# Attention backward for one query: PSUM pools put together, narrower add matmuls, ef matmuls emitted by double units, small stores batched

## The chip, the cores and the metric

The kernel runs on one core of a Trainium2 chip. The metric is device time in microseconds (us), median of several runs. The kernel before takes 953.49 us over 13 runs (951.75 to 955.58). "PE" is the matmul engine (TensorE), "PEld" its weight load, "DVE" the vector engine, "ACT" the scalar engine, "SP" the engine that issues DMA. Runs are labelled fast or slow (slow here: over 1.5% above the fastest run of the same kernel). The "granted clock" is the share of its full speed at which PE was let run, as the trace records it.

## The reference

One query per head against 8192 keys, 32 heads, head size 128, bf16; the output and the gradients of q, k and v.

```python
def _fwd_reference(q, k, v):            # q (1,32,1,128), k and v (1,32,8192,128)
    scale = q.shape[-1] ** -0.5
    scores = jnp.einsum('bhqd,bhkd->bhqk', q, k) * scale
    attn = _softmax(scores, axis=-1)
    return jnp.einsum('bhqk,bhkd->bhqd', attn, v)

def reference(q, k, v, grad_out):       # forward value, then the gradients of q, k, v
    ...
```

k and v are read once (134 MB together) and their gradients written once (134 MB).

## The kernel before

A head needs these steps. DVE multiplies the tile of k by q (`prod`, 4.4 us) and adds the two halves of each row (`h1`, 2.3 us). PE adds the remaining 64 columns with an identity matrix ("adds", output `sp`), and DVE reduces that to the scores. The same is done for v and grad_out. Then comes the softmax: a maximum over partitions with a matmul, `exp` on ACT, a sum with a matmul, a reciprocal. The probabilities and score gradients are put into padded tiles (`ap`, `dp`) and transposed by PE (`tp`). "cd" are 128 small matmuls that give the output and the gradient of q. "ef" are 32 matmuls of 4 rows each whose results, copied from PSUM by ACT, are the gradients of v and k.

The parts that the change and the argument touch (cuts marked by `...`):

```python
    NB = 4                                   # columns per row and add matmul
    ps_sp, ps_tp, ps_cd, ps_st = ...         # four PSUM pools, bufs=1, one bank each
    ps_ef = ctx.enter_context(tc.tile_pool(name="ps_ef", bufs=2, space=bass.MemoryType.PSUM))  # 2 banks each

    def emit_ef_unit(h, u):
        ...
        r = 2 * half + rr
        ef = ps_ef.tile([P, 2, 4 * D], F32, tag="ef")
        for ti in range(2):
            t = 2 * tpair + ti
            nc.tensor.matmul(
                ef[:, ti, :], lhsT=d["adT"][32 * t:32 * t + 4, which, r, :],
                rhs=bd[32 * t:32 * t + 4, :, :],
                start=True, stop=True, tile_position=(32 * t, 0),
            )
        ...
        nc.scalar.activation(out=ost[...], in_=ef[...], func=ACT.Copy)

    for i in range(H + 1):
        ...
        for u in range(4):
            if prv is not None:
                emit_ef_unit(prv, u)                  # two ef matmuls, then 32 cd matmuls
                emit_cd(prv, u // 2, 2 * (u % 2))
                emit_cd(prv, u // 2, 2 * (u % 2) + 1)
        ...
```

The framework reorders: each engine's order of issue comes from a scheduler, not from the text.

## Time and profile before

| | share of the span |
|---|---|
| PE busy | 77% |
| DVE busy | 60% |
| ACT busy | 54% |
| granted PE clock, mean | 0.61 of full speed |
| DMA | 285 GB/s, with stretches of over 400 |

First, lines of the page of before: its span, the busy times (us, share, count of instructions), and the chain of waits by engine.

```profile
span 951.7 us, 15184 instructions
...
PE 728.5 (77%) x6592; PEld 321.1 (34%) x6592; DVE 566.8 (60%) x680; ACT 517.4 (54%) x577; POOL 4.5 (0%) x18
...
PE 49%; DVE 31%; issue 6%; ACT 4%; ACTq 0%; DVEq 0%
```

No engine is full, and the chain changes hands between PE and DVE: it is a loop of waits. The timeline of a middle head (start us, duration us, engine, line, what, and in brackets the idle time ahead with its releaser) shows it:

```profile
477.19 0.29 DVE L164 TENSOR_REDUCE nb<-stt 128x1 f32<-128x128 f32 x1 [1.09 <-PE stt L158]
...
477.40 4.41 DVE L113 TENSOR_TENSOR prod<-kt,qb_all 128x8192 bf16<-128x8192 bf16 x1
...
482.07 2.28 DVE L117 TENSOR_TENSOR h<-prod 128x4096 bf16<-128x4096 bf16 x1
...
484.40 3.57 PE L127 MATMUL sp<-h,ident_bf 128*128 128x256 bf16 x16 [4.81 <-DVE h L117]
...
487.91 0.61 PE L254 MATMUL ef<-gbd,adT 4*128 4x512 bf16 x4
...
497.54 0.61 PE L254 MATMUL ef<-qbd,adT 4*128 4x512 bf16 x2
...
502.94 0.42 DVE L231 COPY cd_sb<-cd 128x256 f32<-128x256 f32 x1 [4.33 <-PE cd L221]
```

DVE leads from 477.2 to 484.4 us while PE runs out of work (4.81 us idle before the adds). Then PE leads for 22 us. The copy of cd comes every 29.38 us (473.56, then 502.94).

PE's busy time within that head by line (window, length, PE busy, PEld busy, granted clock, DMA share, GB/s), in the order ef, cd, adds:

```profile
473.50:502.90 29.40, 9.12 (x32) 1.65 (x32) 0.56 0.71 286
473.50:502.90 29.40, 5.49 (x130) 2.61 (x128) 0.56 0.71 286
473.50:502.90 29.40, 7.63 (x33) 4.42 (x33) 0.56 0.71 286
```

### The profile page before, as it was taken

What the parts mean: (1) busy time and instruction counts of PE and PEld (TensorE: products, weight loads), DVE (VectorE), ACT (ScalarE), POOL (GpSimd) and SP (SyncE); (2) the same over time, 40 slices, a digit from 0 to 9 for tenths busy, and PEclk for the clock granted to TensorE, in tenths of its full rate; (3) what the DMA queues carried; (4) which work ended last, traced back from release to release, by engine and by line L of the source; (5) the groups of instructions that cost most, each with busy time, mean ns of one, the idle gap of its engine ahead of it and who ended that gap; (6) DMA issues with size and microseconds to landing.
All of it is one profiled execution on the core that took longest, in us unless ns stands there. A gap on an engine that the chain in (4) does not pass through costs nothing.

```text
span 951.7 us, 15184 instructions
## 1 busy us (share of the span) xinstructions
PE 728.5 (77%) x6592; PEld 321.1 (34%) x6592; DVE 566.8 (60%) x680; ACT 517.4 (54%) x577; POOL 4.5 (0%) x18
## 2 busy tenths in 40 slices
PE   1598777797777977788777788677797678877696
PEld 0343333343333333333333333333343333333331
DVE  6967775556764567655576555675556765557610
ACT  0066644665445654456554465544565445654487
POOL 1000000000000000000000000000000000000000
PEclk9999655655555555555555555655555655656655
DMA  9588987667777667776677766777767777667355
GB/s 397 220 288 311 377 352 309 274 268 294 292 289 299 253 289 310 287 306 257 274 292 308 310 259 273 287 292 305 288 256 296 299 286 306 256 274 304 127 222 227
DMA packets 28130, 271.52 MB, mean 285 GB/s; under 512 B 3232, under 2 KB 3232, under 8 KB 3232
## 3 DMA queue, kind: packets, MB, share of 16 engines
q1 hardware_dynamic: 27920, 269.51, 70.3%
q8 instruction: 51, 0.84, 0.4%
q10 hardware_dynamic: 144, 1.05, 0.3%
q14 instruction: 15, 0.12, 0.0%
HBM read 136.31 MB, written 134.23 MB: 284 GB/s over the span
## 4 chain that ended last, share of the span: by engine, by line
PE 49%; DVE 31%; issue 6%; ACT 4%; ACTq 0%; DVEq 0%
DVE prod L113 23%; PE ef L254 21%; PE cd L221 14%; PE sp L127 5%; DVE h L117 4%; ACT ost L260 4%; PE stt L232 3%; PE tp L208 2%; PE tp L206 2%; PE stt L158 1%; PE stt L178 1%; DVE nb L164 1%; DVE eda L176 1%; DVE zt L177 0%; DVE ndl L186 0%
## 5 line engine op out<-in xcount | busy, mean ns | idle before, releaser
L260 ACT ACTIVATE ost<-ef 128x1024 bf16<-128x1024 f32 x512 | 505.3, 1025 | 299.9 <-PE ef L254 286.7
L127 PE MATMUL sp<-h,ident_bf 128*128 128x256 bf16 x1024 | 239.1, 400 | 162.5 <-DVE h L117 161.0
L127 PEld LDWEIGHTS <-ident_bf 128*128 128x128 bf16 x1024 | 134.4, 136 | 259.3 <-issue 207.1
L254 PE MATMUL ef<-qbd,adT 4*128 4x512 bf16 x512 | 149.4, 575 | 27.9 <-ACT ost L260 27.0
L117 DVE TENSOR_TENSOR h<-prod 128x4096 bf16<-128x4096 bf16 x64 | 146.0, 2281 | 0.0
L113 DVE TENSOR_TENSOR prod<-kt,qb_all 128x8192 bf16<-128x8192 bf16 x32 | 141.3, 4415 | 3.4 <-DMA kt<-in_k_dram 3.4
L113 DVE TENSOR_TENSOR prod<-vt,gb_all 128x8192 bf16<-128x8192 bf16 x32 | 141.4, 4417 | 0.0
L254 PE MATMUL ef<-gbd,adT 4*128 4x512 bf16 x512 | 134.3, 583 | 2.4 <-ACT ost L260 2.0
L254 PEld LDWEIGHTS <-adT 4*128 4x128 bf16 x1024 | 51.9, 98 | 168.0 <-issue 162.5
L231 DVE COPY cd_sb<-cd 128x256 f32<-128x256 f32 x32 | 13.6, 424 | 133.7 <-PE cd L221 133.7
L144 DVE TENSOR_TENSOR qbd<-mask,qb_all 128x512 bf16<-128x512 bf16 x32 | 13.6, 425 | 89.8 <-PE ef L254 89.8
L210 DVE COPY adT<-tp 128x1024 bf16<-128x1024 bf16 x32 | 22.1, 691 | 41.6 <-PE tp L208 41.6
L234 DVE CAST orow<-stt 1x256 bf16<-1x256 f32 x32 | 13.2, 412 | 48.5 <-PE stt L232 48.5
L232 PE MATMUL stt<-cd_sb,sel_f 128*1 128x256 f32 x64 | 31.9, 601 | 0.0
L221 PE MATMUL cd<-vt,ap__136 128*1 128x128 bf16 x704 | 31.7, 295 | 0.0
L221 PE MATMUL cd<-vt,ap__132 128*1 128x128 bf16 x704 | 31.5, 296 | 0.0
L178 PE MATMUL stt<-zt,ones_f 128*128 128x2 f32 x64 | 15.8, 317 | 19.5 <-DVE zt L177 19.5
L221 PE MATMUL cd<-kt,dp__138 128*1 128x128 bf16 x704 | 30.4, 301 | 0.0
L221 PE MATMUL cd<-kt,dp__134 128*1 128x128 bf16 x704 | 30.3, 301 | 0.0
L221 PE MATMUL cd<-vt,ap__140 128*1 128x128 bf16 x640 | 27.8, 288 | 0.0
L221 PE MATMUL cd<-kt,dp__142 128*1 128x128 bf16 x640 | 27.3, 292 | 0.2 <-issue 0.2
L164 DVE TENSOR_REDUCE nb<-stt 128x1 f32<-128x128 f32 x32 | 9.3, 289 | 29.6 <-PE stt L158 29.5
(278 smaller groups left out, 337.2 us busy)
## 6 DMA issues: line engine op xcount, KB each, us to landing
out_dram<-ost SPq DMA_DIRECT2D x128, 1024.0 KB, 3.9
kt<-in_k_dram SPq DMA_DIRECT2D x32, 2048.0 KB, 15.0
vt<-in_v_dram SPq DMA_DIRECT2D x32, 2048.0 KB, 12.3
gb_all<-in_grad_out_dram ACTq DMA_DIRECT2D x1, 1024.0 KB
qb_all<-in_q_dram SPq DMA_DIRECT2D x1, 1024.0 KB
out_dram<-orow SPq DMA_DIRECT2D x64, 0.2 KB
```

The source lines that it names most:

```text
L113: nc.vector.tensor_tensor(out=prod[:], in0=xt[:], in1=wb[:, h, :].unsqueeze(1).to_broadcast([P, J, D]), op=ALU.mult)
L117: nc.vector.tensor_tensor(out=h1[:], in0=prod[:, :, 0:DH], in1=prod[:, :, DH:D], op=ALU.add)
L127: nc.tensor.matmul(d["sp"][:, which, :, :], lhsT=ident_bf[:], rhs=prod[:, :, a * NB:(a + 1) * NB], start=(a == 0), stop=(a == NA - 1),)
L164: nc.vector.tensor_reduce(out=nb[:], in_=stt[:, 0:P], axis=AX.X, op=ALU.max, negate=True)
L178: nc.tensor.matmul(stt[:, P:P + 2], lhsT=ones_f[:], rhs=zt[:], start=True, stop=True)
L206: nc.tensor.transpose(tp[:, 0, r, :], apad[:, r, :], ident_bf[:])
L208: nc.tensor.transpose(tp[:, 1, r, :], dpad[:, r, :], ident_bf[:])
L210: nc.vector.tensor_copy(out=adT[:], in_=tp[:])
L221: nc.tensor.matmul(cd[32 * jj:32 * jj + 1, which * D:(which + 1) * D], lhsT=pad[:, r, c:c + 1], rhs=xt[:, j, :], start=(r == 0 and t == 0) ...
L232: nc.tensor.matmul(d["st"][0:1, 256:512], lhsT=sel_f[:], rhs=cd_sb[:], start=True, stop=True)
L254: nc.tensor.matmul(ef[:, ti, :], lhsT=d["adT"][32 * t:32 * t + 4, which, r, :], rhs=bd[32 * t:32 * t + 4, :, :], start=True, stop=True, ti ...
L260: nc.scalar.activation(out=ost[:, j0:j0 + 8, :].rearrange("p j d -> p (j d)"), in_=ef[:].rearrange("p a n -> p (a n)"), func=ACT.Copy,)
```

## The change

Its intent is to free PSUM banks for a third ef buffer, to emit ef matmuls four at a time, and to drop 64 stores of 256 bytes. The scores' sums and cd now share one bank (`pa`), the transposes and statistics another (`pb`). To make the scores' sums fit, an add matmul has 128 columns instead of 256, so there are twice as many.

```diff
-    NB = 4
+    NB = 2
-    ps_sp, ps_tp, ps_cd, ps_st ...   (four pools, bufs=1)
-    ps_ef = ... bufs=2
+    ps_ab = ... bufs=1
+    ps_ef = ... bufs=3
+    pa = ps_ab.tile([P, 512], F32, tag="pa")
+    sp_v = pa[:, 0:2 * J * NB].rearrange("p (w j b) -> p w j b", w=2, b=NB)
+    cd = pa[:, 256:512]
+    pb = ps_ab.tile([P, 512], F32, tag="pb")          # transposes, statistics
+    outT = consts.tile([P, 2, H], F32, tag="outT")    # both small outputs, stored once at the end
...
-        nc.tensor.matmul(d["st"][0:1, 256:512], lhsT=sel_f[:], rhs=cd_sb[:], start=True, stop=True)
-        ... two stores of 256 bytes per head
+        for w_ in range(2):
+            nc.tensor.matmul(pb[:, 384 + w_:385 + w_], lhsT=cd_sb[:, w_ * D:(w_ + 1) * D], rhs=sel_f[:], ...)
+        nc.vector.tensor_copy(out=outT[:, :, h], in_=pb[:, 384:386])
...
-    def emit_ef_unit(h, u):          # two matmuls, one buffer
+    def emit_ef_du(h, du):           # four matmuls, two buffers, then two evictions
+        for tpair in range(2):
+            ef = ps_ef.tile([P, 2, 4 * D], F32, tag="ef")
+            for ti in range(2):
+                t = 2 * tpair + ti
+                nc.tensor.matmul(ef[:, ti, :], ..., tile_position=(32 * t, 0))
+        for tpair in range(2):
+            nc.scalar.activation(...)
...
+            for du in range(2):
+                emit_ef_du(prv, du)
+                for r in range(4):
+                    emit_cd(prv, du, r)               # 64 cd matmuls in a row
```

The transposes of `dp` now wait for the copy of those of `ap`, since both use the same part of `pb`.

## The prediction

> **What bounds the kernel now.** No engine is full: the page gives PE 77%, DVE 60%, ACT 54% of 951.7 us, and DMA moves 285 GB/s where single stretches reach over 410. The chain of waits says a loop: PE 49%, DVE 31%. A middle head in the timeline (473.5 to 502.9 us, 29.4 us per head) splits into DVE-only work of 7.2 us (nb, product of k, reduce, half-add, while PE idles 4.8 us until the half-add ends) and 22.2 us of PE (adds, ef, transposes, cd, adds). PE runs at granted clock 0.5 almost throughout. Copies of cd come 28.4 us apart on average, since early heads have a better order.
>
> **What the change does.**
> - Adds: 64 matmuls of 128 columns per head for 32 of 256. Columns are equal. The trace spaces 256-column adds 223 ns (3.57 us for 16); the Trainium skill ("TensorE: Matmul & The Clock Gate", Back-to-back issue gap) says N/1.2 ns cold, 213, and the trace agrees within 5%. Transposes, also 128 columns with a 128-column weight load each, come every 135 ns. So a pair of small adds should cost 225 to 270 ns: 0 to +1.5 us of PE per head.
> - Reductions read half as much: 0.42 to about 0.29 us, twice per head.
> - The sum over cd: one matmul pair of 0.94 us becomes two with full-width f32 weights; the 128x2 f32 matmul of the statistics takes 0.52, so about 1.04: no gain.
> - 64 tiny stores vanish. They are in no chain: about 0.
> - A third ef buffer: "PE ef waits for ACT ost" is 29 us in total; at most that.
> - sp and cd now share one bank, tp and statistics another. The skill ("PSUM — Partial Sum Buffer", Terms) says PE and DVE may not touch one bank and quadrant at once; so dependencies order them (no run shows the collision itself). This, and the new emission, changes the static order, which I read from the built program.
>
> **The new loop, per head**, counted with durations of the trace from the last cd matmul: ef, cd sum and 32 adds of s, with interleaved ef: 7.1 to 7.9 us. Then DVE alone leads: reduce 0.3, half-add 2.25, max, product of v 4.4, dmx, reduce, half-add 2.25, nb: to about 17.7. Exp now stands on ACT behind all eight ef evictions of dk (1.025 us each), which end at 17 to 19.4. Exp, eda, zt: 0.8. Then the next product of k, 4.4 us, stands in DVE's order ahead of the reciprocal that only needs the sum, so the transposes start at 23.5 to 25.2 while PE idles some 4 us. Transposes with a copy between, 8 us with cd and four ef pairs. Period 31 to 33.3 us against 28.4: both products and both half-adds (13.3 us) are now in series with s-adds, softmax and cd, where before about half were hidden behind PE.
>
> First cd ends at about 54 us as before; 31 periods of 32.2, less 9 in the last heads without products, plus 15 of tail: about 1055 us.
>
> **Prediction:** 1050 us, range 1000 to 1090; faster by over 2%: 0.05, within 2%: 0.05, slower by over 2%: 0.90.
>
> **What would show it.** PE idle per head rising from 5 to 8-10 us, in two gaps: before the transposes (on ap, behind the product of k) and before the statistics matmul (on zt). Exp waiting with ACT busy until just before. Chain: DVE share above 45%. Adds 112 to 135 ns apart. "PE ef waits for ACT ost" falling or unchanged. DVE waits before cd_sb remaining.
>
> **What would make it wrong.** A PE clock at full speed for long after the denser adds (period below 30); adds of 4-byte runs slower than 135 ns; k or v loads arriving late (then longer).

## More of the kernel before

`tile_position=(32 * t, 0)` puts a matmul on one of four row groups of the array.

## The result

The changed kernel takes 911.07 us (907.95 to 917.35, 8 runs); the ratio to before is 0.956 (95% interval 0.9538 to 0.9581). A ratio is the mean time of one kernel's fast runs over that of the other's fast runs in the same rounds, so not quite the ratio of the medians quoted here. The prediction, 1050 us, was wrong, and wrong in sign.

The page of after, the same lines where it has them:

```profile
span 906.1 us, 17304 instructions
...
PE 629.7 (69%) x7682; PEld 410.0 (45%) x7682; DVE 567.4 (63%) x715; ACT 501.6 (55%) x577; POOL 4.5 (1%) x18
...
PE 3%; ACT 1%; DVE 0%; ACTq 0%; issue 0%; DVEq 0%
```

The chain of waits stops early here (its shares sum to some 4%), so it can't be compared; the timeline has to do. One head of after, from one copy of cd to the next (488.96 to 516.26). Down to 504.15 the lines are of this head; from 478.16 on they are the steps of the head before it, which this head repeats:

```profile
488.96 0.42 DVE L230 COPY cd_sb<-pa 128x256 f32<-128x256 f32 x1 [3.66 <-PE pa L220]
...
489.44 0.61 PE L232 MATMUL pb<-sel_f,cd_sb 128*128 128x1 f32 x4 [0.21 <-DVE cd_sb L230]
...
489.90 1.04 PE L128 MATMUL pa<-h,ident_bf 128*128 128x128 bf16 x8
...
493.61 1.04 PE L128 MATMUL pa<-h,ident_bf 128*128 128x128 bf16 x8
...
494.69 0.29 DVE L136 TENSOR_REDUCE t__5634<-pa 128x64 f32<-128x128 f32 x1 [0.50 <-PE pa L128]
...
497.23 4.42 DVE L116 TENSOR_TENSOR prod<-vt,gb_all 128x8192 bf16<-128x8192 bf16 x1
...
504.15 0.28 DVE L165 TENSOR_REDUCE nb<-pb 128x1 f32<-128x128 f32 x1
...
478.16 4.41 DVE L116 TENSOR_TENSOR prod<-kt,qb_all 128x8192 bf16<-128x8192 bf16 x1
...
478.39 0.56 PE L179 MATMUL pb<-zt,ones_f 128*128 128x2 f32 x2 [2.33 <-DVE zt L178]
...
483.13 0.61 PE L208 MATMUL pb<-ident_bf,ap__127 128*128 128x128 bf16 x4 [4.18 <-DVE ap__127 L192]
...
484.77 0.61 PE L254 MATMUL ef<-gbd,adT 4*128 4x512 bf16 x4
...
485.32 1.55 PE L220 MATMUL pa<-vt,ap__127 128*1 128x128 bf16 x51
...
487.34 1.55 PE L220 MATMUL pa<-kt,dp__129 128*1 128x128 bf16 x64
...
488.83 0.39 PE L254 MATMUL ef<-gbd,adT 4*128 4x512 bf16 x3
```

The static order is just the one that the prediction read from the built program: DVE goes through reduction, half-add, product of v and nb in one piece, then the product of k stands ahead of the reciprocal, and PE waits for the transposes. Here are that wait and the one on the statistics matmul, totals over the run (who waited for what: us, times, longest):

```profile
PE pb L179 <- DVE zt L178: 79.2, 32, 8.7
...
PE pb L208 <- DVE ap__123 L192: 42.5, 11, 4.2
PE pb L208 <- DVE ap__127 L192: 42.1, 11, 4.2
PE pb L208 <- DVE ap__131 L192: 41.8, 10, 4.2
...
PE ef L254 <- ACT ost L261: 33.2, 67, 0.5
```

The new wait ahead of the transposes is 126 us in all, 4.2 us in a head like this one. But the copies of cd come every 27.31 us (this one, then 488.96 above), not every 32.2:

```profile
461.65 0.42 DVE L230 COPY cd_sb<-pa 128x256 f32<-128x256 f32 x1 [3.66 <-PE pa L220]
```

Cut into the prediction's own terms, with the times of the lines above:

| stretch of a head | predicted, us | measured, us |
|---|---|---|
| last cd matmul to end of the adds of s | 7.1 to 7.9 | 5.7 (488.9 to 494.6) |
| end of the adds to end of nb | 9.8 to 10.6 | 9.8 (494.65 to 504.43) |
| end of nb to product of k | 0.8 to 2.5 | 1.0 (477.13 to 478.16) |
| product of k to transposes | 5.0 | 5.0 (478.16 to 483.13) |
| transposes to last cd matmul | 8 | 5.7 (483.13 to 488.83) |

The second and third row are worked out from the points of time that the prediction gives (17.7 for the end of nb; 17 to 19.4 for ACT, and 0.8 more). The terms in which DVE leads lie in the predicted ranges, two of them at the low end. The two stretches in which PE leads were oversized by some 4 us together. PE's busy time by line in one head of after, in the order ef, cd, adds:

```profile
461.65:488.96 27.31, 6.00 (x35) 1.21 (x32) 0.63 0.79 308
461.65:488.96 27.31, 3.69 (x128) 2.93 (x128) 0.63 0.79 308
461.65:488.96 27.31, 8.05 (x64) 6.53 (x64) 0.63 0.79 308
```

Against before, ef fell from 9.12 to 6.00 us, cd from 5.49 to 3.69, and the adds rose from 7.63 to 8.05. In after, what follows four ef matmuls starts 0.54 to 0.55 us after them (484.77 to 485.32, 486.80 to 487.34), where in before two took as long (497.54 to 498.07).

### The profile page after: what moved, and what is told of

It reads as the page before. It is cut to its first block, busy times and chain, and to the rows that moved or that the text cites. A ratio compares the mean times of both kernels' runs of the same rounds, so it can differ in the third digit from the quotient of the medians.

```text
span 906.1 us, 17304 instructions
## 1 busy us (share of the span) xinstructions
PE 629.7 (69%) x7682; PEld 410.0 (45%) x7682; DVE 567.4 (63%) x715; ACT 501.6 (55%) x577; POOL 4.5 (1%) x18
## 5 line engine op out<-in xcount | busy, mean ns | idle before, releaser
L128 PE MATMUL pa<-h,ident_bf 128*128 128x128 bf16 x2048 | 257.3, 288 | 23.0 <-DVE h L120 23.0
L128 PEld LDWEIGHTS <-ident_bf 128*128 128x128 bf16 x2048 | 209.6, 120 | 83.4 <-issue 81.8
L254 PE MATMUL ef<-qbd,adT 4*128 4x512 bf16 x512 | 110.4, 471 | 33.2 <-ACT ost L261 33.2
L254 PE MATMUL ef<-gbd,adT 4*128 4x512 bf16 x512 | 84.8, 550 | 0.0
L179 PE MATMUL pb<-zt,ones_f 128*128 128x2 f32 x64 | 17.7, 346 | 79.2 <-DVE zt L178 79.2
L209 DVE COPY adT<-pb 128x512 bf16<-128x512 bf16 x64 | 27.2, 425 | 29.2 <-PE pb L208 29.2
L208 PE MATMUL pb<-ident_bf,ap__123 128*128 128x128 bf16 x44 | 6.7, 308 | 42.5 <-DVE ap__123 L192 42.5
L208 PE MATMUL pb<-ident_bf,ap__127 128*128 128x128 bf16 x44 | 6.7, 308 | 42.1 <-DVE ap__127 L192 42.1
L208 PE MATMUL pb<-ident_bf,ap__131 128*128 128x128 bf16 x40 | 6.1, 308 | 41.8 <-DVE ap__131 L192 41.8
L159 PE MATMUL pb<-dmx,ones_f 128*128 128x128 f32 x64 | 25.4, 500 | 0.9 <-DVE dmx L157 0.9
L232 PE MATMUL pb<-sel_f,cd_sb 128*128 128x1 f32 x128 | 19.8, 259 | 6.7 <-DVE cd_sb L230 6.7
L220 PE MATMUL pa<-vt,ap__127 128*1 128x128 bf16 x704 | 24.0, 306 | 0.0
L220 PE MATMUL pa<-vt,ap__123 128*1 128x128 bf16 x704 | 23.5, 307 | 0.0
```

The lines of the kernel that those rows point to most:

```text
L128: nc.tensor.matmul(d["sp"][:, which, :, :], lhsT=ident_bf[:], rhs=prod[:, :, a * NB:(a + 1) * NB], start=(a == 0), stop=(a == NA - 1),)
L159: nc.tensor.matmul(stt[:, 0:P], lhsT=ones_f[:], rhs=dmx[:], start=True, stop=True)
L179: nc.tensor.matmul(stt[:, P:P + 2], lhsT=ones_f[:], rhs=zt[:], start=True, stop=True)
L208: nc.tensor.transpose(tp_v[:, r, :], pad_[:, r, :], ident_bf[:])
L209: nc.vector.tensor_copy(out=adT[:, w_, :, :], in_=tp_v)
L220: nc.tensor.matmul(cd[32 * jj:32 * jj + 1, which * D:(which + 1) * D], lhsT=pad[:, r, c:c + 1], rhs=xt[:, j, :], start=(r == 0 and t == 0) ...
```

## The experiments

Theory Q: four ef matmuls that stand next to each other on PE and sit on four different row groups run at the same time, so a four costs what a two cost. The prediction costed each two at 0.54 us. The Trainium skill ("TensorE: Matmul & The Clock Gate", Part 3: Packing small matmuls — row/col tiling) says that matmuls on different row groups run concurrently; the trace of after agrees, 0.54 us for four. Rivals: the third ef buffer as such or the batched stores (B), a higher granted clock under the denser adds (C), the emission by itself (E).

### The same kernel with two row groups used twice

```diff
-        for tpair in range(2):                  # t = 0,1 then 2,3 of one r
-            ef = ps_ef.tile(...)
+        for rr in range(2):                     # t, t+1 of r, then t, t+1 of r + 1
+            r = 2 * half + rr
+            ef = ps_ef.tile(...)
```

> The kernel after, with one edit: the four ef matmuls of a double unit use two row groups of the array twice (tiles t, t+1 of two r) instead of four row groups once. Same counts, same order on PE, DVE and ACT, same buffers. Theory Q (four ef matmuls in different row groups run at once, 0.54 us for four instead of 0.54 for two): each run of four costs 1.06 us, about 2 us more per head on the PE stretches that lead, up to 3 with the ACT queue behind it: 970 to 1000 us. Rival B (the gain comes from the third ef buffer, the batched stores or the shorter reductions): unchanged, 905 to 917. Rival C (the gain comes from a higher granted clock under the denser adds): unchanged, 905 to 920, clock 0.64 as before.

Measured: 1003.14 us, ratio to before 1.052 (1.0496 to 1.0544). The order on all engines is that of after: in the built programs no instruction of PE, DVE, ACT or SP stands elsewhere. In its timeline:

```profile
473.57 1.03 PE L254 MATMUL ef<-gbd,adT 4*128 4x512 bf16 x4
...
474.54 1.55 PE L220 MATMUL pa<-vt,ap__131 128*1 128x128 bf16 x51
...
476.02 1.03 PE L254 MATMUL ef<-gbd,adT 4*128 4x512 bf16 x4
...
476.99 1.88 PE L220 MATMUL pa<-kt,dp__133 128*1 128x128 bf16 x64
```

A four now takes 0.97 us (473.57 to 474.54) instead of 0.54. Rivals B and C fall as causes by themselves: buffers, stores and adds were untouched, and 92 us came back. The time is even 3 us over the expected range. One thing was not expected: the run of 64 cd matmuls takes 1.81 us here (476.99 to 478.80) and 1.49 in after, though it wasn't edited. That is the granted clock, taken up below: the edit took away the fours, and the raised clock went with them. So not all of the 92 us is the fours; the table under "Why the prediction was wrong" divides them.

### New pools, old emission

```diff
-    emit_ef_du, loop by double units            (as in after)
+    emit_ef_unit, loop by single units          (as in before, with eight 128-column adds for four of 256)
```

> The kernel after (pools, 128-column adds, batched stores) with the old emission of ef units one by one, cd and adds in between; the static order of DVE is that of after, on PE ef comes in twos and cd in runs of 16 to 32. Theory Q: as slow as or a little slower than a_noquad, 975 to 1010 us, that is slower than before: without the fours, the shared bank alone loses. Rival B: 905 to 920.

Measured: 1009.09 us, ratio 1.0584 (1.0568 to 1.0601). The shared banks, narrower adds, third buffer and batched stores together, without the fours, are slower than before. This is close to what the prediction described.

### Old pools, new emission

```diff
-    emit_ef_unit, loop by single units
+    emit_ef_du, loop by double units            (all else as in before)
```

> The kernel before (five pools, two ef buffers, 256-column adds, small stores) with the new emission alone. The built program keeps the order of before: ef in twos between runs of 14 cd matmuls, since the scheduler spreads them when only two ef buffers exist and cd has its own bank. Theory Q: the emission alone brings nothing: 940 to 960 us. Rival E (the emission is the gain): 905 to 920.

Measured: 954.52 us, ratio 1.0007 (0.9986 to 1.0027). The text asks for fours, but the built program has them in twos, with runs of about 14 cd matmuls in between. Emission alone changes nothing here (rival E falls), because the scheduler undoes it. Fours with separate banks and two buffers were thus never run.

### cd back in a bank of its own

```diff
-    ps_ef ... bufs=3
+    ps_ef ... bufs=2
-    cd = pa[:, 256:512]
+    pc = ps_ab.tile([P, 512], F32, tag="pc")
+    cd = pc[:, 256:512]
```

> The kernel after with cd in a bank of its own and so two ef buffers instead of three. The built program goes back to the order of before (ef in twos, DVE: product of k after nb). Theory Q with the shared bank as what sets the order: 940 to 985 us. Rival: the shared bank is a cost that the change pays and the gain lies elsewhere: faster than 905.

Measured: 951.38 us, ratio 0.9982 (0.9964 to 0.9999). The built program goes back to the order of before (product of k behind nb, ef in twos). A build with two ef buffers and the bank still shared, not run, keeps the order of after (on DVE in all 759 places, on PE in all but 93 of 7594); so it is the shared bank that makes the scheduler choose it. The Trainium skill ("PSUM — Partial Sum Buffer", Terms) says that two engines may not use one bank and quadrant at once; in the built program DVE's reads and PE's writes of the shared bank wait for each other. No run here shows a collision.

### The order pinned: a control, and three single edits

From here on the order of after was written out by hand and pinned on every engine, since small edits had let the scheduler reorder everything. A block at the end of the kernel ties each instruction to the one before it on its engine:

```diff
+    for ins in nc.cur_bb.bb.instructions:
+        if ins.engine in prev:
+            tc.add_manual_dep(ins, prev[ins.engine].name, info, reason="order of the text")
+        prev[ins.engine] = ins
```

> Control for the next three: the kernel after, emitted in the order that its built program has in a middle head, with that order pinned on every engine, so that one edit no longer lets the scheduler reorder the rest. Expected as after: 900 to 920 us.

Measured: 917.21 us (three fast runs of 914.6 to 917.3 and one slow of 933.5), ratio 0.9622 (0.9603 to 0.9642). The control stands 0.7% above after with the same order in a middle head. Its trace is that of the slow run and is not used for comparisons.

```diff
-    ps_ef ... bufs=3
+    ps_ef ... bufs=2
```

> p_after with two ef buffers instead of three, order pinned. Theory Q: a run of four needs two free buffers at once; with two in all, each run waits for both evictions of the run before, and those in the cd stretch come after 2 us, so 0.5 to 1 us are lost per run on the leading stretches: 935 to 980 us. Rival (the third buffer brings nothing, as the wait of ef for ACT is only about 30 us in total in both traces): 900 to 920.

Measured: 996.36 us, ratio 1.0465 (1.0449 to 1.048), 79 us above its control and 16 above the expected range. The order is unchanged, only the buffer is gone:

```profile
500.82 1.27 PE L288 MATMUL ef<-gbd,adT 4*128 4x512 bf16 x4
...
502.02 1.88 PE L243 MATMUL pa<-t__4295,dp__125 128*1 128x128 bf16 x64
```

The second four of the cd stretch, at 500.82, now takes 1.20 us to the next start instead of 0.54: it falls apart while it waits for evictions. Here too some of the 79 us is the clock: the heads are 30.07 us at half clock, where heads with three buffers at half clock take 28.47 (p_dummystores, below). That is 1.6 us per head for the buffer itself, some 50 us in all by estimate, not much less than the 2.0 us of the fours, since without it not every four holds. The wait of ef for ACT was a poor guide: it totals 28.9 us in before, 33.2 in after and only 44.4 in this run.

```diff
         nc.vector.tensor_copy(out=outT[:, :, h], in_=pb[:, 384:386])
+        nc.sync.dma_start(out=o0v[h:h + 1, :], in_=qb_all[0:1, h, :])
+        nc.sync.dma_start(out=o1v[h:h + 1, :], in_=qb_all[0:1, h, :])
```

> p_after with two extra stores of 256 bytes per head on the same queue as the loads and the large stores, as before had them (their content is overwritten at the end). Theory: small stores are in no chain: 900 to 922 us, within 1% of p_after. Rival (batching them is a good part of the gain): 930 or more.

Measured: 912.94 us, ratio 0.958 (0.9563 to 0.9597), not slower than its control. Batching the stores is no measurable part of the gain, as predicted. This run has a second use. Its copies of cd, all in one fast run, don't come evenly:

```profile
710.37 0.42 DVE L253 COPY cd_sb<-pa 128x256 f32<-128x256 f32 x1 [3.65 <-PE pa L243]
...
737.68 0.42 DVE L253 COPY cd_sb<-pa 128x256 f32<-128x256 f32 x1 [3.65 <-PE pa L243]
...
765.31 0.42 DVE L253 COPY cd_sb<-pa 128x256 f32<-128x256 f32 x1 [3.99 <-PE pa L243]
...
793.78 0.42 DVE L253 COPY cd_sb<-pa 128x256 f32<-128x256 f32 x1 [3.97 <-PE pa L243]
...
820.61 0.42 DVE L253 COPY cd_sb<-pa 128x256 f32<-128x256 f32 x1 [2.89 <-PE pa L243]
```

Heads of 27.31, 27.63, 28.47 and 26.83 us stand next to each other with the same instructions. What differs is the granted clock in the cd stretch and just behind it: 0.50 from 789.0 to 793.8 us, and 1.00 from 819.4 to 820.6. The run of 64 cd matmuls in the head of 28.47 us:

```profile
791.86 1.88 PE L243 MATMUL pa<-t__8207,dp__125 128*1 128x128 bf16 x64
```

That is 1.80 us (to the next start, 793.66), and 0.99 us at 819.50 in the head of 26.83 us. The times of equal matmuls agree with the recorded clock here, and a head moves with it by up to 1.6 us.

```diff
     def back(h):
-        if ok(h + 2):
-            emit_mult(h + 2, 0)
         emit_st_fin(h)
         emit_tp(h, 0)
         emit_cd(h, 0, 0, 13)
         emit_tp(h, 1)
+        if ok(h + 2):
+            emit_mult(h + 2, 0)
```

> p_after with one move: on DVE the product of k of head h+2 stands behind the second copy of adT of head h instead of ahead of the reciprocal. Theory: the product is what PE waits for before the transposes (4.2 us per head), and 4.4 us fit into the stretch in which DVE waits for cd: period from 27.3 to about 23.5 us, 785 to 815 us. Rival (the product only moves the wait to the copy of cd, and the loop is bound elsewhere, by ACT or the loads): gain under 2 us per head, 850 us or more.

Measured: 842.51 us, ratio 0.8848 (0.8835 to 0.8861). The gain is real, 75 us against the control, but lies between the theory (100 to 130) and the rival (under 64). The timeline of one head says where the rest went:

```profile
368.14 0.17 DVE L207 RECIPROCAL rz<-pb 128x1 f32<-128x1 f32 x1 [0.74 <-PE pb L201]
...
370.87 4.42 DVE L117 TENSOR_TENSOR prod<-t__4295,qb_all 128x8192 bf16<-128x8192 bf16 x1
...
372.73 1.06 PE L243 MATMUL pa<-t__3651,dp__129 128*1 128x128 bf16 x64
...
375.20 0.42 DVE L253 COPY cd_sb<-pa 128x256 f32<-128x256 f32 x1
...
375.67 1.01 PE L260 MATMUL pb<-sel_f,cd_sb 128*128 128x1 f32 x4 [1.28 <-DVE cd_sb L253]
```

PE no longer waits 4.2 us for the transposes, but DVE waits 0.74 us for the sum before the reciprocal, and the product of k ends at 375.2 us, 1.5 us after the last cd matmul (373.7), so the copy of cd is late and the sum over cd waits 1.28 us. The period is 24.6 to 25.2 us. The expectation (27.3 less 4.2, "about 23.5") had left 0.4 us for such waits.

### The clock

```diff
     def back(h):
+        scr = ps_ef.tile([P, 2, 4 * D], F32, tag="ef", name="scr")
+        for _ in range(8):
+            nc.tensor.matmul(scr[:, 0, :], lhsT=ident_bf[:], rhs=qb_all[:, 0:4, :], start=True, stop=True)
```

> p_after with eight extra 128x512 matmuls into a free ef buffer in the gap in which PE waits for the transposes (3.4 us of a 4.2 us gap at half clock); nothing reads them. Theory H (part of the miss is the granted clock: PE's dense adds and cd runs raise it in some windows, and where it is raised in the cd stretch a head is 27.3 us, where it isn't 28.4): with the gap filled the clock is up in the cd stretch in every head, granted clock over 0.7, 870 to 905 us. Rival (the clock of that stretch is worth nothing, or the extra matmuls only delay): 910 to 935.

Measured: 913.83 us, ratio 0.959 (0.9574 to 0.9606), granted clock 0.62. The theory as worded fell: filling the gap with dense work did not raise the clock in every cd stretch. It was 0.50 from 422.0 to 430.5 us of its trace, though in the head before it the 64 cd matmuls at 404.08 took 1.00 us. What raises it when is not settled here. That the granted clock in the cd stretch goes with the length of a head is shown by p_dummystores; what would hold it up is open.

The recorded clock needs a check against times. In a_noquad it reads 1.00 from 100 to 200 us, yet a four takes 0.96 us there (108.65 to 109.61) as it does at a recorded 0.50, and heads on both sides are 30.50 us. One run of a_oldemit is recorded at 1.0 and took 1009.32 us, the others at 0.51 to 0.52 and 1008.82 to 1009.28. The mean of a run is therefore a weak figure; the stretches used above are those in which the times agree with it.

### Block width alone

```diff
-    NB = 2
+    NB = 4        (in the kernel with cd in its own bank and two ef buffers)
```

> The same kernel as a_nb2_cdbank_ef2 (951 us, order of before) with 256-column adds: only the block width differs, and the order is nearly the same. Theory (width costs 0.4 us of PE busy per head or less, hidden or not): 940 to 955. Rival (narrow adds raise the clock and so are a gain): 965 or more here.

Measured: 947.48 us, ratio 0.9935 (0.9914 to 0.9955), against 951.38 with narrow adds. The two were timed in different rounds, so their ratios to before are compared, 0.9935 with 0.9982: the narrow adds cost about 0.5% in that order, with all else nearly in the same place. They are no gain. They were the price of fitting the sums beside cd.

### A version that beats both

The chain suggests its own repair: keep the fours and the third buffer, and put DVE's large products where PE works on cd and adds.

```diff
-    h1p bufs=2, NPAD = 3, cd_sb, dmx and adT with bufs=3
+    h1p bufs=3, NPAD = 2, cd_sb and dmx with bufs=1, adT with bufs=2
     DVE, one head:
-    cd_sb, outT, gbd, reduce s, half k, max, prod v, dmx, reduce d, half v, nb, qbd, eda, zt, prod k, rz, ..., adT
+    cd_sb, outT, prod k, half k, reduce s, max, dmx, prod v (half), nb, prod v (half), gbd, reduce d, eda, zt, rz, ..., adT, half v, qbd
     PE: the max matmul right behind its dmx, two ef fours behind the adds and behind the sum matmul
```

> A version from what the runs so far say: fours of ef and three ef buffers kept, order pinned, DVE's large products moved to where PE works on cd and adds: reduction of s, max and dmx at once after the adds, product and half-add of k of the next head between the copy of cd and that reduction, product of v in two halves with nb between them, half-add of v after the copies of adT (a third half-add buffer, paid with smaller pools). Theory (the loop is a chain of DVE and PE, no engine is full): period about 21 to 23 us, 720 to 790 us. Rival (the loads and stores bind: 8.4 MB per head at the 410 to 450 GB/s that busy stretches show are 19 to 21 us): 740 or more with waits of products for loads.

Measured: 755.72 us, ratio 0.7931 (0.7913 to 0.795), correct. One head of it, 22.09 us (window, length, busy of PE, PEld, DVE, ACT, POOL, granted clock, DMA share, GB/s):

```profile
404.74:426.83 22.09, 19.24 (x243) 12.73 (x240) 17.98 (x24) 15.72 (x19) 0.00 (x0) 0.65 0.97 375
```

The DMA engines are busy 97% of the head, at 375 GB/s. The time lies in the ranges of both theories, so the trace has to decide. The rival had named a sign of its own, products that wait for loads, and the trace lacks it: the products waited for a load once, 2.7 us at the start, and the chain that ended last is 57% PE, 35% DVE and 2% DMA. Little room is left in the DMA engines, but nothing in the trace says that they set the time. Which part of the edit gave how much was not tested.

## Why the prediction was wrong

**Right.** The order of after, read from the built program, was on the chip as described: product of k ahead of the reciprocal, PE idle 4.2 us before the transposes and 2.3 before the statistics matmul, DVE's stretches in the ranges counted. The adds came 121 ns apart, inside the stated 112 to 135. The stores were worth nothing that could be measured. And without the fours the new structure is indeed slower than before (1003 and 1009 us): the direction of that reading was right, for a kernel that isn't the one that was built.

**The step that failed** is "8 us with cd and four ef pairs" and "with interleaved ef: 7.1 to 7.9 us", that is PE's share of the loop. The miss per head is 32.2 less 27.31, 4.9 us. The runs divide it so:

| part | us per head | from |
|---|---|---|
| fours on four row groups, counted as two twos each | 2.0 | a_noquad 30.50 less 28.47 of p_dummystores, both at half clock in the cd stretch |
| granted clock raised late in the cd stretch and behind it | 1.2 | heads of 28.47 and 27.31 in p_dummystores, one order |
| the rest: cd in runs of 51 and 64 rather than 14, the sum over cd, ACT's queue ahead of exp | 1.7 | 32.2 less 30.50, by subtraction |

For the rest, cd is the largest part: at 0.52 us for 14 matmuls (37 ns each) the 115 of the leading stretch would come to 4.3 us (the prediction gives only the 8 us of the whole stretch), and in a_noquad they took 1.48 and 1.81, 3.3 us. The two matmuls of the sum over cd took 0.46 us at the raised clock (489.44 to 489.90) and 0.88 in a_noquad, where 1.04 was counted. The prediction had named a faster clock as what would make it wrong ("period below 30"); that happened, but it is the smaller part, and why the clock rose is not shown.

**A second step that failed:** "A third ef buffer: ... 29 us in total; at most that." Taking it away from the pinned kernel cost 79 us, some 50 of them without the clock (estimate above). A sum of waits bounds what a buffer is worth only if nothing else uses it; here it is what lets four matmuls start together.

**What the trace of before already showed.** Its timeline has four ef matmuls in 0.61 us at 487.91 us, where ACT had left both buffers free, and two in 0.61 us everywhere else. The prediction took the common line as the cost of two matmuls.

**Where the gain comes from.** Not from any one part: emission alone 954, pools and narrow adds with old emission 1009, all without the third buffer 996, all without the row groups 1003, all together 911. The bank sharing buys the third buffer, and costs the serial order of DVE; the fours, with the raised clock that came with them, pay more than that back. p_kafter and p_best show how much that order still held back.

## What to carry to other kernels

Cost small matmuls by the group in which they will stand on PE, not one by one: look in the trace for the places where a group happens to run together, and count the row groups and free PSUM buffers that this takes. When a change moves the order, compare the orders of the built programs before timing, and pin the order before testing single edits. Look for a long operation that stands ahead of a short one that others wait for: here moving one product took the kernel from 917 to 843 us, and moving both with their neighbours, two of the ef fours and some buffer counts took it to 756.

## What the Trainium skill lacked or had wrong

- "TensorE: Matmul & The Clock Gate", Part 3, has the concurrency of row groups, but no figure for a group of four that a pipelined kernel breaks up. The runs show 0.54 us for a four that stands together, 0.54 for each two where cd matmuls stand between them (a_oldemit, 475.06 to 475.60), 0.97 for a four on two row groups, and 1.20 for a four with a PSUM buffer missing.
- The same page, Part 1, says that sustained PE activity of about 3.4 us raises the clock. Here it stayed at half in before while PE was busy, by the profile, in every microsecond of an 11 us stretch of ef and cd matmuls; the times agree (two ef matmuls take 0.61 us there and 0.39 at 519.54). In p_warm it stayed so in the head at 422 us through 3.4 us of 128x512 matmuls and the stretch behind them, and rose in the head before. Whether matmuls as small as ef and cd count as activity no run here shows. The line of before (columns as above):

```profile
492.00:503.00 11.00, 11.00 (x157) 4.33 (x155) 2.02 (x8) 9.99 (x11) 0.00 (x0) 0.50 0.64 261
```

- The same page, Back-to-back issue gap, gives about 81 ns for a sustained pair of weight load and 128-column matmul. The transposes agree where the clock is full: in p_best four of them, from 420.82 to 421.15, come 82 ns apart at clock 1.00 (135 at half clock, in before at 492.00). The adds of after, also 128 columns with a weight load each, don't: they come 121 ns apart both at the full and at the half clock (eight from 489.90 to 490.88 and from 493.61 to 494.58). So it isn't the weight load alone that holds them. They read their moving operand in runs of 4 bytes, and the transposes in whole rows; whether that is the reason no run shows. The granted clock of those two microseconds:

```profile
489.90:490.90 1.00, 1.00 (x11) 0.79 (x10) 0.16 (x1) 0.43 (x1) 0.00 (x0) 1.00 1.08 459
493.60:494.60 1.00, 1.00 (x14) 0.79 (x11) 0.43 (x1) 0.88 (x1) 0.00 (x0) 0.50 0.81 279
```

- The same page, Part 1, gives a free-running clock window of 3413 ns. By estimate with this figure, the 27.31 us of after are 8.00 of them, and in the profiled run most heads keep that period to 0.01 us. Other traces in which the clock comes and goes repeat a longer pattern of head lengths, and it too is a whole number of windows: three heads of p_kafter take 75.07 us (21.99), eight of p_warm 218.46 us (64.00), eleven of p_best 245.75 us (72.00). In a_noquad, mostly at half clock, the 30.50 us of a head are 8.94. No page says that a loop can lock to that window. These numbers suggest it; no run here proves it.
